# Sliding-window attention feeding a routed expert layer: attention's transfers issued at other places of a step, and the gate's value logits in four matmuls of 128 keys by 64 columns

## The chip, the cores and the metric

The kernel runs on 1 core of one Trainium2 chip. The metric is device time of one execution in microseconds (us). The kernel before takes 1083.74 us, the median of 3 runs (1080.22 to 1085.4).

Names of the engines: PE is TensorE's matmul, PEld its weight load, DVE VectorE, ACT ScalarE, POOL GpSimd; SP is SyncE, which here only issues transfers.

## The reference

Attention over 8 batches, 8 heads, 576 positions of 64 channels, where a query sees the 64 keys up to its own; its output, as 4608 rows of 512 channels, goes through a layer of 8 experts, of which each row uses the two with the highest noisy logits.

```python
scores = q @ k.T / sqrt(64)                       # only 0 <= query - key < 64 count
attn = softmax(scores);  x = attn @ v             # all float32
logits = x @ w_gate + log1p(exp(x @ w_noise)) * noise
top2, weights = softmax over the two largest logits of a row
out[row] += weight * (relu(x[row] @ w1[e]) @ w2[e])     # for both experts e of the row
```

## The kernel before

**Two stages.** Attention runs in NT = 36 steps of one Python loop (`for j in range(NT + 3)`, three more to drain it), and after it the experts run over lists of rows: for each expert three chunks of 384, 448 and 384 rows, first an up product (`up`), then a down product (`down`), each float32 value split into two parts that the fast matmul form takes. Every engine executes its instructions in the order in which the program emits them, so the order of the calls in the loop is the order on each engine. Nothing else schedules.

**A step of attention.** Step j has one block of 64 positions (i = j // 4) of one pair of batches (bp = j % 4), all 8 heads. In the loop's order: `scores(j)` (PE, queries by keys of this block and the one before), `soft_b(j-1)` and `soft_a(j)` (ACT: the exponential, and a copy out of PSUM), `pv(j-2)` (PE, probabilities by values), `norm_b(j-3)` (ACT, 8 scaled copies), `soft_max(j)`, `soft_max2(j)` (DVE, then POOL's subtraction), `transp(j-1)` (PE), `logits(j)` (PE), `apply_mask(j-1)` (DVE) and `logits_copy(j)` (ACT). On PE a step from the fifth on is 16 matmuls of scores, 32 of pv, 4 transposes and 8 of logits; float32 matmuls, transposes aside, are executed as two passes, each with a weight load of its own, so that the profile counts 32, 64, 4 and 16.

**Logits through the values.** The gate's logits x @ [w_gate, w_noise] need x, but x = attn @ v, so the program multiplies the values by the gate first. `logits(j)` takes the transposed values of the step (`vt`, 128 channels of two heads by four blocks of 128 keys) as the stationary operand and the gate's columns (`wgx_sb`) as the moving one: for each block and each half a of its keys a matmul with 64 stationary columns and 32 moving ones, into 64 of the 128 partitions of a PSUM tile `ps_g` (`VG`). Two places of 128 columns alternate between steps. `logits_copy(j)` copies 128 x 128 values from there into slot 4 of the value tile `vw`, and `pv` two steps later multiplies all of `vw` by the probabilities. `ps_g` is also where the routing's small matmuls go (`rank`, `reserve`).

**Transfers.** A step loads queries (`qc`), keys (`KW`), values (`vw`) and transposed values (`vt`), 256 KB each (values 272 KB), and stores one block of rows (`xrows`, 256 KB). All are issued by SP from one queue, in order; SP stops at a transfer until its own conditions hold, and what stands behind it waits with it. Every transfer also waits for the landing of the one eight places before it. At the head of step j stand the loads of queries and keys for step j+3 and of `vt` for step j+2, then `store(j-4)`, then at some steps one of five small things (`REST`), and at steps 2, 4, 6 and 8 a quarter of the first expert's weights (`load_w1`, 512 KB). The values for step j+2 stand behind `pv(j-2)`, which frees their place. `qc` has four buffers, `vt` three.

**After attention** the rows' slots are scattered and rows gathered by POOL (`scatter`, `gather`), which drains a list of such calls, two or three a step (`drain_slots`).

Of the kernel before, what the change touches and what calls it, by code (L numbers as in the profile page):

```python
# [8 lines left out]
F32 = mybir.dt.float32  # L9
# [4 lines left out]
AF = mybir.ActivationFunctionType  # L14
# [3 lines left out]
B, H, S, D = 8, 8, 576, 64  # L18
N, DM, E, F = 4608, 512, 8, 1024
NB = S // 64  # L20
NP = B // 2
NT = NP * NB
KD, KF = DM // 128, F // 128
# [11 lines left out]
W1G = 12  # L35
# [28 lines left out]
def tile_kernel(ctx, tc, qT, kT, vx, vT, wgx, noise, w1, w2, out):  # L64
    nc = tc.nc
# [14 lines left out]
    acon = at.enter_context(tc.tile_pool(name="acon", bufs=1))  # L80
    ld = at.enter_context(tc.tile_pool(name="ld", bufs=2))
# [3 lines left out]
    KW = acon.tile([128, NP, 2, H, 64], F32)  # L85

    VW = [acon.tile([128, 2, 5, 2, 4, 17], F32, name=f"vw{j}") for j in range(NP)]
    QC, VT = {}, {}

    def load_qk(j):  # L90
        i, bp = divmod(j, NP)
        QC[j] = ld.tile([128, H, 64], F32, name="qc", bufs=4)
        nc.sync.dma_start(QC[j], qT[bp, :, i])
        nc.sync.dma_start(KW[:, bp, i % 2], kT[bp, :, i])


    def load_v(j):
        i, bp = divmod(j, NP)
        nc.sync.dma_start(VW[bp][:, i % 2, 0:4], vx[bp, i])


    def load_vt(j):
        i, bp = divmod(j, NP)
        VT[j] = ld.tile([128, 4, 128], F32, name="vt", bufs=3)
        nc.sync.dma_start(VT[j], vT[bp, i])

    for j in range(2):
        load_qk(j)
    wgx_sb = acon.tile([128, 4, 32], F32)
    nc.sync.dma_start(wgx_sb, wgx)  # L110
    load_vt(0)
    load_v(0)
    load_qk(2)
    load_vt(1)
    load_v(1)
    load_qk(3)

    ones = acon.tile([128, 128], F32)
    nc.vector.memset(ones, 1.0)

    idle = ps.tile([128, 512], F32, name="ps_g")

    def warm(n):
        for _ in range(n):
            nc.tensor.matmul(idle[:, 384:512], lhsT=ones, rhs=ones, start=True, stop=True)
# [43 lines left out]
    def load_pads(q):  # L169
        if q == 0:  # L170
            o = LIST * 2
            for n in CHUNKS:
                w = n // 32 * 2
                nc.sync.dma_start(rows(L, o, [[w, 32], [LIST * 2, E - 1], [1, w]]),
                                  pad_f[:, None, :w].to_broadcast([32, E - 1, w]))
                o += n * 2
            return
        pad_t = pad_o.rearrange("k p c -> k (p c)")
        if q == 1:
            nc.sync.dma_start(rows(L, 0, [[256, CAP // 128], [1, 256]]), pad_t[:CAP // 128])  # L180
            nc.sync.dma_start(rows(L, CAP // 128 * 256, [[256, 1], [1, CAP % 128 * 2]]), pad_t[:1, :CAP % 128 * 2])
        else:
            nc.sync.dma_start(rows(L, CAP * 2, [[256, OVT], [LIST * 2, E], [1, 256]]),
                              pad_t[:, None, :].to_broadcast([OVT, E, 256]))

    REST = [lambda: nc.sync.dma_start(noise_sb, noise), lambda: nc.sync.dma_start(X[0:DUMP, :], zero),
            lambda: load_pads(0), lambda: load_pads(1), lambda: load_pads(2)]
# [5 lines left out]
    w1s = wts.tile([128, KD, F], F32)  # L193
# [2 lines left out]
    w1l = wts.tile([128, KD, F], F32R)  # L196
    W2 = {}

    def load_w1(e, ks=slice(0, KD)):
        if e < E:  # L200
            nc.sync.dma_start(w1s[:, ks], w1[e][:, ks])

    def load_w2(e, ks=slice(0, KF)):
        if e < E:
            nc.sync.dma_start(w2s[:, ks], w2[e][:, ks])
# [10 lines left out]
        return [lambda f=f: split(w2s[:, f], W2["h"][:, f], W2["l"][:, f]) for f in range(KF)]  # L216


    VG = idle[:, 0:256].rearrange("p (n c) -> p n c", n=2)

    def logits(j):
        p = VG[:, j % 2]
        x = VT.pop(j)
        for u in range(2):
            for g in range(2):
                for a in range(2):
                    q = u * 2 + g
                    nc.tensor.matmul(p[a * 64:a * 64 + 64, q * 32:q * 32 + 32], lhsT=x[:, q, a * 64:a * 64 + 64],
                                     rhs=wgx_sb[:, g * 2 + a, :], start=True, stop=True)

    def logits_copy(j):
        i, bp = divmod(j, NP)
        nc.scalar.activation(VW[bp][:, i % 2, 4, :, :, 0:16].rearrange("p u k e -> p (u k) e"),
                             VG[:, j % 2].rearrange("p (k e) -> p k e", e=16), AF.Copy)

    ST, T, P, TP, PT, XT = {}, {}, {}, {}, {}, {}

# [340 lines left out]
    def turn(e, c):  # L578
        pool = (exa, EXB.get("p"))[work.index((e, c)) % 2]
        xh = pool.tile([128, KD, WIDE], F32R, name="xh")  # L580
        xl = pool.tile([128, KD, WIDE], F32R, name="xl")
        XH[e, c], XL[e, c] = xh, xl
        cur = {}

        def f(q, m):
            if e:
                y = exa.tile([128, m // 32, KD, 32], F32, name="xy", bufs=2)
                nc.vector.transpose(y.rearrange("p t k c -> p (t k c)"),
                                    XG[e, c, q][:, :m // 32].rearrange("p t d -> p (t d)"))
                cur[q] = y.rearrange("p t k c -> p k t c")  # L590
            else:
                y = turn_bank()[:, :KD * m].rearrange("p (k m) -> p k m", k=KD)
                for k in range(KD):
                    nc.tensor.transpose(y[:, k], XG[e, c, q][:m, k * 128:k * 128 + 128], ident[:m, :m])
                cur[q] = y.rearrange("p k (t c) -> p k t c", c=32)

        def g(q, m):
            h, l = (x[:, :, q * 128:q * 128 + m].rearrange("p k (t c) -> p k t c", c=32) for x in (xh, xl))
            nc.scalar.activation(h, cur[q], AF.Copy)  # L599
            nc.vector.tensor_tensor(l, cur[q], h.bitcast(F32), op=OP.subtract)  # L600
        return [lambda q=q, m=m, x=x: x(q, m) for q, m in tiles(c) for x in (f, g)]
# [90 lines left out]
    def drain(n):  # L692
        calls[0] += 1
        while n and pending and calls[0] > calls[1]:
            f = next(pending[0], None)
            if f == HOLD:
                calls[1] = calls[0] + f
            elif f:
                f()
                n -= 1  # L700
            else:
                pending.pop(0)
# [5 lines left out]
    def drain_slots(n):  # L708
        for f in slots[:n]:
            f()  # L710
        del slots[:n]
# [4 lines left out]
    def ahead(n):  # L716
        for _ in range(n):
            if j >= NT and len(taken) < AHEAD:
                next(up00)
                taken.append(1)  # L720


    def rate(q):
        n = next(b for a, b in RATE if j < a)
        return (q + 1) * n // SLOTS - q * n // SLOTS
# [5 lines left out]
    def on(f, j, *a):  # L731
        if 0 <= j < NT:
            f(j, *a)

    for j in range(NT + 3):
        if j == TURN:
            for q, f in enumerate(turn(0, 0)):
                aux.setdefault(j + q // 2, []).append(f)
        if 0 < j < NT - 3:
            load_qk(j + 3)  # L740
        if j < NT - 2:
            load_vt(j + 2)
        if j < 2:
            load_v(j + 2)
        on(store, j - 4)
        if 2 < j < 3 + len(REST):
            REST[j - 3]()
        if W1G - 8 <= 2 * j < W1G - 8 + 4 * KD and j % 2 == 0:
            k = (j * 2 - W1G + 8) // 4
            load_w1(0, slice(k, k + 1))  # L750
        if NT - 2 <= j < NT + 2:
            load_w2(0, slice((j - NT + 2) * 2, (j - NT + 3) * 2))
        on(norm_a, j - 3)
        drain(rate(0))
        on(scores, j)
        on(soft_b, j - 1)
        on(soft_a, j)
        ahead(2)
        drain(rate(1))
        on(pv, j - 2)  # L760
        on(norm_b, j - 3, 0)
        on(soft_max, j)
        on(soft_max2, j)
        drain_slots(1)
        if j < NP:
            warm(WARM)
        on(transp, j - 1)
        ahead(2)
        on(logits, j)
        on(norm_b, j - 3, 1)  # L770
        on(apply_mask, j - 1)
        drain(rate(2))
        on(logits_copy, j)
        ahead(2)
        on(gate, j - 3)
        drain(rate(3))
        drain_slots(1 + j % 2)
        for f in aux.get(j, ()):
            f()
        drain(rate(4))  # L780
# [13 lines left out]
    for n, (e, c) in enumerate(work):  # L794
# [29 lines left out]
        if last and e + 1 < E:  # L824
            side += split_w1() + [lambda: load_w1(e + 2)]
# [5 lines left out]
        if n == 1:  # L831
            load_w1(1)
# [62 lines left out]
    with tc.If(ntot > 0):  # L895
# [4 lines left out]


_INS = {"qT": [NP, 128, NB, H, 64], "kT": [NP, 128, NB, H, 64], "vx": [NP, NB, 128, 4, 2, 4, 17],
        "vT": [NP, NB, 128, 4, 128], "wgx": [128, 4, 32], "noise": [128, NT, E], "w1": [E, 128, KD, F], "w2": [E, 128, KF, DM]}


def layout(inputs):
# [46 lines left out]
```

## Time and profile before

| what | value |
|---|---|
| median of 3 runs | 1083.74 us |
| the profiled execution | 1081.11 us, of which its span is 1079.3 us |
| PE busy over the span | 1004.2 us, 93% |
| PE matmuls, and as many weight loads | 8313 |
| DVE, ACT, POOL busy | 444.0, 391.4, 534.3 us |
| attention, to the last transposes of its loop | about 190 us |

The page gives one profiled execution. Times in rows are microseconds from the span's start. In a group of instructions, "out<-in" are the program's names, the number after x is the count, then busy time, mean of one in nanoseconds, and idle time of the engine just before those instructions with what ended it. "issue" as the one who ended an idle time means that the engine waited for nothing that the profile shows. Matmuls are pipelined, so the busy time of neighbours overlaps, and the pace is read from the starts.

### The profile page before, as it was taken

The numbers are of one execution on the slowest core, as the hardware profiler recorded it, in microseconds if no ns is written. First come the engines' busy times: TensorE is split into PE (matmuls) and PEld (weight loads), VectorE is DVE, ScalarE is ACT, GpSimd is POOL, SyncE is SP. The second block draws the span as 40 slices with busy tenths as digits, with TensorE's granted clock in tenths as the row PEclk, the third lists the DMA queues.
The fourth block names the chain that finished last, engine by engine and source line by source line (L and its number), as shares of the span: only waits on it lengthen the run. The fifth ranks groups of instructions, "written<-read, shape, count | busy, mean of one in ns | idle before, by whom it ended". The sixth has DMA issues, their size and how long they took to land. (4 is left out here: it accounts for less than half of the span.)

```text
span 1079.3 us, 20457 instructions
## 1 busy us (share of the span) xinstructions
PE 1004.2 (93%) x8313; PEld 894.3 (83%) x8313; DVE 444.0 (41%) x943; ACT 391.4 (36%) x975; POOL 534.3 (50%) x612
## 2 busy tenths in 40 slices
PE   8778777899969999999999999999999999999994
PEld 7667566778859888988898988898889888998893
DVE  6687768531234224422543253326232623352220
ACT  4775656521233224322432252225222522342220
POOL 4435636664276524653465446544555454554411
PEclk9998989999989999999999999999999999999997
DMA  9998988498634324423442345234422542233212
GB/s 347 331 324 225 253 222 245 102 252 177 188 118 132 57 39 125 132 50 42 120 132 49 44 118 136 46 52 123 128 48 46 156 102 42 47 54 51 39 22 32
DMA packets 62681, 133.45 MB, mean 124 GB/s; under 512 B 16776, under 2 KB 17266, under 8 KB 60786
## 3 DMA queue, kind: packets, MB, share of 16 engines
q1 hardware_dynamic: 39986, 92.11, 26.9%
q0 software_dynamic: 22592, 39.95, 21.5%
q8 instruction: 67, 1.10, 0.4%
q14 instruction: 36, 0.29, 0.1%
HBM read 92.31 MB, written 39.70 MB: 122 GB/s over the span
## 5 line engine op out<-in xcount | busy, mean ns | idle before, releaser
L573 POOL DMA_INDIRECT xg<-xrows,ixs x266 | 258.6, 972 | 81.1 <-issue 74.7
L640 PE MATMUL ps_u<-xh,w1h 128*128 128x384 f32 (+1 forms) x752 | 260.7, 347 | 11.5 <-ACT xh L599 10.3
L641 PE MATMUL ps_u<-xl,w1h 128*128 128x384 f32 (+1 forms) x752 | 260.5, 346 | 0.0
L642 PE MATMUL ps_u<-xh,w1l 128*128 128x384 f32 (+1 forms) x752 | 260.1, 346 | 0.0
L655 POOL DMA_INDIRECT out_dram<-yo,lts x70 | 111.6, 1594 | 298.9 <-ACT yo L675 154.0
L670 PE MATMUL ps_d<-w2h,hh 128*128 128x512 f32 x576 | 224.7, 390 | 0.0
L672 PE MATMUL ps_d<-w2h,hl 128*128 128x512 f32 x576 | 224.5, 390 | 0.0
L671 PE MATMUL ps_d<-w2l,hh 128*128 128x512 f32 x576 | 224.4, 390 | 0.0
L647 DVE SCALAR_TENSOR_TENSOR hl<-ps_u,hh 128x384 fp32r<-128x384 f32 x188 | 104.7, 557 | 270.9 <-ACT hh L646 270.9
L646 ACT ACTIVATE hh<-ps_u 128x384 fp32r<-128x384 f32 x188 | 92.4, 492 | 240.7 <-PE ps_u L642 240.5
L640 PEld LDWEIGHTS ps_u<-xh,w1h 128*128 128x128 f32 x752 | 142.1, 189 | 17.3 <-ACT xh L599 11.2
L641 PEld LDWEIGHTS ps_u<-xl,w1h 128*128 128x128 f32 x752 | 141.9, 189 | 5.2 <-DVE xl L600 0.7
L642 PEld LDWEIGHTS ps_u<-xh,w1l 128*128 128x128 f32 x752 | 141.9, 189 | 3.7
L670 PEld LDWEIGHTS ps_d<-w2h,hh 128*128 128x128 f32 x576 | 108.1, 188 | 22.8 <-issue 1.1
L672 PEld LDWEIGHTS ps_d<-w2h,hl 128*128 128x128 f32 x576 | 108.1, 188 | 22.6
L671 PEld LDWEIGHTS ps_d<-w2l,hh 128*128 128x128 f32 x576 | 108.1, 188 | 21.8
L675 ACT ACTIVATE yo<-ps_d,lts 128x512 f32<-128x512 f32 x63 | 43.4, 688 | 194.9 <-PE ps_d L672 115.4
L600 DVE TENSOR_TENSOR xl<-xy,xh 128x512 fp32r<-128x512 f32 (+1 forms) x70 | 46.7, 667 | 147.7 <-ACT xh L599 147.7
L475 POOL DMA_INDIRECT slots<-val,posi x72 | 70.1, 974 | 18.6 <-issue 14.1
L316 PE MATMUL ps_o<-vw,pt 64*64 64x85 f32 x2176 | 56.7, 248 | 21.4 <-issue 20.2
L281 POOL TENSOR_TENSOR t<-t,mx 128x512 f32<-128x512 f32 x36 | 37.5, 1042 | 78.0 <-DVE mx L280 74.5
L316 PEld LDWEIGHTS ps_o<-vw,pt 64*64 64x64 f32 x2176 | 51.3, 143 | 25.4 <-issue 23.9
(145 smaller groups left out, 950.1 us busy)
## 6 DMA issues: line engine op xcount, KB each, us to landing
w2s<-in_w_dram SPq DMA_DIRECT2D x7, 2048.0 KB
w1s<-in_w_dram SPq DMA_DIRECT2D x7, 2048.0 KB
vw<-in_vx_dram SPq DMA_DIRECT2D x36, 272.0 KB
out_dram<-zero SPq DMA_DIRECT2D x37, 256.0 KB
qc<-in_qT_dram SPq DMA_DIRECT2D x36, 256.0 KB
KW<-in_kT_dram SPq DMA_DIRECT2D x36, 256.0 KB
vt<-in_vT_dram SPq DMA_DIRECT2D x36, 256.0 KB
xrows<-x SPq DMA_DIRECT2D x36, 256.0 KB
```

Of the source, the lines that this page charges most:

```text
L316: nc.tensor.matmul(PO[j][u * 64:u * 64 + 64, a, g * 2 + x, :], lhsT=pt[pa, w, u * 2 + g, x * 64:x * 64 + 64], rhs=v[pa, (i + w) % 2, :, u, ...
L475: s = nc.gpsimd.indirect_dma_start(out=L, out_offset=bass.IndirectOffsetOnAxis(ap=posi[:, c2, q:q + 1], axis=0), in_=val[:, c2, q, :], in_ ...
L573: nc.gpsimd.indirect_dma_start(out=XG[e, c, t // 4][:, t % 4, :], out_offset=None, in_=XQ[:(DUMP + seen.get((e, c), NT) * 128) * 4], in_of ...
L640: nc.tensor.matmul(p[:, :n], lhsT=w1h[:, k, fs], rhs=xh[:, k, :n], start=(k == 0), stop=False)
L641: nc.tensor.matmul(p[:, :n], lhsT=w1h[:, k, fs], rhs=xl[:, k, :n], start=False, stop=False)
L642: nc.tensor.matmul(p[:, :n], lhsT=w1l[:, k, fs], rhs=xh[:, k, :n], start=False, stop=(k == KD - 1))
L646: nc.scalar.activation(h, p[:, :main], AF.Relu)
L647: nc.vector.scalar_tensor_tensor(l, p[:, :main], 0.0, h.bitcast(F32), op0=OP.max, op1=OP.subtract)
L655: nc.gpsimd.indirect_dma_start(out=out[:DUMP + seen.get((e, c), NT) * 128], out_offset=bass.IndirectOffsetOnAxis(ap=LT[e, c][:m, q, 0:1], ...
L670: nc.tensor.matmul(p, lhsT=hh[f][:, sl], rhs=w2h[:, f, :], start=(f == 0), stop=False)
L671: nc.tensor.matmul(p, lhsT=hh[f][:, sl], rhs=w2l[:, f, :], start=False, stop=False)
L672: nc.tensor.matmul(p, lhsT=hl[f][:, sl], rhs=w2h[:, f, :], start=False, stop=(f == KF - 1))
```

## The change

**Logits.** One matmul for each block of 128 keys, with all 128 as the stationary columns and 64 moving columns, those of both halves. Half of the result is not wanted; the two copies take the wanted halves, one for each half of the partitions. There is one place of 256 columns instead of two of 128. `wgx_sb` holds the same numbers in another shape.

**Transfers.** Of step j's head only the keys and the store are left. The queries for step j+3 are issued behind `scores(j)`, the transposed values for j+2 behind `logits(j)`, `qc` has three buffers and `vt` two, so both loads now take the place that the matmuls just before them have read. The quarters of the weights become halves of quarters (256 KB) at steps 2 to 9, behind the queries.

```diff
+    def load_q(j):
+        i, bp = divmod(j, NP)
+        QC[j] = ld.tile([128, H, 64], F32, name="qc", bufs=3)
+        nc.sync.dma_start(QC[j], qT[bp, :, i])
+    def load_k(j):
+        i, bp = divmod(j, NP)
+        nc.sync.dma_start(KW[:, bp, i % 2], kT[bp, :, i])
...
-        VT[j] = ld.tile([128, 4, 128], F32, name="vt", bufs=3)
+        VT[j] = ld.tile([128, 4, 128], F32, name="vt", bufs=2)
...
-    VG = idle[:, 0:256].rearrange("p (n c) -> p n c", n=2)
+    VG = idle[:, 0:256].rearrange("p (n c) -> p n c", n=1)
...
-                for a in range(2):
-                    q = u * 2 + g
-                    nc.tensor.matmul(p[a * 64:a * 64 + 64, q * 32:q * 32 + 32], lhsT=x[:, q, a * 64:a * 64 + 64],
-                                     rhs=wgx_sb[:, g * 2 + a, :], start=True, stop=True)
+                q = u * 2 + g
+                nc.tensor.matmul(p[:, q * 64:q * 64 + 64], lhsT=x[:, q, :], rhs=wgx_sb[:, g], start=True, stop=True)
...
-        nc.scalar.activation(VW[bp][:, i % 2, 4, :, :, 0:16].rearrange("p u k e -> p (u k) e"),
-                             VG[:, j % 2].rearrange("p (k e) -> p k e", e=16), AF.Copy)
+        for a in range(2):
+            h = slice(a * 64, a * 64 + 64)
+            nc.scalar.activation(VW[bp][h, i % 2, 4, :, :, 0:16].rearrange("p u (g x) e -> p (u g) x e", x=2),
+                                 VG[h, 0].rearrange("p (k a x e) -> p k a x e", a=2, x=2, e=16)[:, :, a], AF.Copy)
...
         if 0 < j < NT - 3:
-            load_qk(j + 3)
-        if j < NT - 2:
-            load_vt(j + 2)
+            load_k(j + 3)
+        on(store, j - 4)
...
         on(scores, j)
+        if j < NT - 3:
+            load_q(j + 3)
+        if W1G // 2 - 4 <= j < W1G // 2 + 4:
+            k = j - W1G // 2 + 4
+            load_w1(0, slice(k // 2, k // 2 + 1), slice(k % 2 * F // 2, (k % 2 + 1) * F // 2))
+        if 2 < j < 3 + len(REST):
+            REST[j - 3]()
...
         on(logits, j)
+        if j < NT - 2:
+            load_vt(j + 2)
```

SP's order of before around steps 6 and 7 (each row a transfer; "waits PE" or "waits Activation" is a condition on that engine, "DMAHW" one on a landing):

```order
L93 DMA qc<-in_qT_dram 128x512 [waits DMAHW4_49,PE_49]
L94 DMA KW<-in_kT_dram 128x512 [waits DMAHW5_49]
L105 DMA vt<-in_vT_dram 128x512 [waits DMAHW6_49,PE_49]
L338 DMA xrows<-x 128x512 [waits DMAHW7_49,Activation_49]
L180 DMA slots<-pad_o 9x256 [waits DMAHW0_49,Pool_49]
L181 DMA slots<-pad_o 1x128 [waits DMAHW1_49]
L201 DMA w1s<-in_w_dram 128x1024 [waits DMAHW2_49]
L99 DMA vw_90<-in_vx_dram 128x544 [waits DMAHW3_49,PE_49]
L93 DMA qc<-in_qT_dram 128x512 [waits DMAHW4_49]
L94 DMA KW<-in_kT_dram 128x512 [waits DMAHW5_49]
L105 DMA vt<-in_vT_dram 128x512 [waits DMAHW6_49,PE_49]
L338 DMA xrows<-x 128x512 [waits DMAHW7_49,Activation_49]
```

The same place now:

```order
L112 DMA vt<-in_vT_dram 128x512 [waits DMAHW5_49,PE_49]
L97 DMA KW<-in_kT_dram 128x512 [waits DMAHW6_49]
L345 DMA xrows<-x 128x512 [waits DMAHW7_49,Activation_49]
L93 DMA qc<-in_qT_dram 128x512 [waits DMAHW0_49,PE_49]
L208 DMA w1s<-in_w_dram 128x512 [waits DMAHW1_49]
L187 DMA slots<-pad_o 9x256 [waits DMAHW2_49,Pool_49]
L188 DMA slots<-pad_o 1x128 [waits DMAHW3_49]
L106 DMA vw_90<-in_vx_dram 128x544 [waits DMAHW4_49,PE_49]
L112 DMA vt<-in_vT_dram 128x512 [waits DMAHW5_49,PE_49]
L97 DMA KW<-in_kT_dram 128x512 [waits DMAHW6_49]
L345 DMA xrows<-x 128x512 [waits DMAHW7_49,Activation_49]
L93 DMA qc<-in_qT_dram 128x512 [waits DMAHW0_49,PE_49]
```

Before, one transfer of a step (the values, `vw`) and the next step's store wait for an engine and the others follow at once; now the queries, the values, the transposed values and the store each wait for a different place of the step.

PE's order of before in one step (scores, pv, transposes, logits):

```order
L257 MATMUL ps_s<-KW,qc 64x128 [waits DMAHW1_49,DMAHW0_49,DVE_49]
L257 MATMUL ps_s<-KW,qc 64x128 x15
L316 MATMUL ps_o<-vw_90,pt 64x85 [waits DMAHW7_49,DVE_49,Activation_49]
L316 MATMUL ps_o<-vw_90,pt 64x85 x31
L293 MATMUL ps_t<-ident,p 128x128 [waits PE_49,Activation_49]
L293 MATMUL ps_t<-ident,p 128x128 x3
L228 MATMUL ps_g<-wgx_sb,vt 64x32 [waits DMAHW7_49]
L228 MATMUL ps_g<-wgx_sb,vt 64x32 x7
```

and now:

```order
L264 MATMUL ps_s<-KW,qc 64x128 [waits DMAHW1_49,DMAHW0_49,DVE_49]
L264 MATMUL ps_s<-KW,qc 64x128 x15
L323 MATMUL ps_o<-vw_90,pt 64x85 [waits DMAHW6_49,DVE_49,Activation_49]
L323 MATMUL ps_o<-vw_90,pt 64x85 x31
L300 MATMUL ps_t<-ident,p 128x128 [waits PE_49,Activation_49]
L300 MATMUL ps_t<-ident,p 128x128 x3
L234 MATMUL ps_g<-wgx_sb,vt 128x64 [waits DMAHW4_49]
L234 MATMUL ps_g<-wgx_sb,vt 128x64 x3
```

Eight matmuls became four at the same place. On ACT one copy became two at the same place; DVE's and POOL's orders are the same.

## Rows read from the trace of the kernel before

**Rows 1.** Stretches: length, busy time of each engine (count), clock, DMA share, GB/s.

```profile
19.79:171.06 151.27, 115.27 (x3282) 99.81 (x3281) 109.38 (x282) 98.95 (x357) 73.44 (x105) 0.93 0.93 279
25.40:68.40 43.00, 33.46 (x1012) 29.22 (x1012) 32.60 (x73) 32.50 (x118) 20.15 (x25) 0.96 0.98 337
68.40:105.00 36.60, 27.96 (x770) 24.13 (x771) 27.54 (x78) 22.62 (x83) 16.81 (x26) 0.91 0.85 238
400.00:600.00 200.00, 200.00 (x990) 180.19 (x989) 75.24 (x137) 66.01 (x132) 102.75 (x94) 1.00 0.38 90
```

**Rows 2.** Groups by line, PE's matmuls in 19.79 to 171.06 us.

```profile
L316 PE MATMUL ps_o<-vw,pt 64*64 64x85 f32 x1792 | 48.0, 251 | 21.4 <-issue 20.2 <-ACT vw L233 0.7 <-DMA vt<-in_vT_dram 0.2
L257 PE MATMUL ps_s<-KW,qc 64*64 64x128 f32 x903 | 36.1, 292 | 7.7 <-issue 7.7
L228 PE MATMUL ps_g<-wgx_sb,vt 128*64 128x32 f32 x464 | 20.6, 230 | 3.6 <-issue 3.6
```

**Rows 3.** Timeline of PE: start, duration, instruction, count, idle time before it.

```profile
48.53 0.45 PE L257 MATMUL ps_s<-KW,qc 64*64 64x128 f32 x8 [1.77 <-issue]
48.75 1.41 PE L316 MATMUL ps_o<-vw,pt 64*64 64x85 f32 x64
50.09 0.66 PE L293 MATMUL ps_t<-ident,p 128*128 128x128 f32 x4
50.67 0.66 PE L228 MATMUL ps_g<-wgx_sb,vt 128*64 128x32 f32 x16
51.26 1.10 PE L257 MATMUL ps_s<-KW,qc 64*64 64x128 f32 x32
52.42 0.33 PE L316 MATMUL ps_o<-vw,pt 64*64 64x85 f32 x2
53.93 1.40 PE L316 MATMUL ps_o<-vw,pt 64*64 64x85 f32 x62 [1.17 <-issue]
```

**Rows 4.** The page's part 1: busy time, share and instructions of each engine.

```profile
PE 1004.2 (93%) x8313; PEld 894.3 (83%) x8313; DVE 444.0 (41%) x943; ACT 391.4 (36%) x975; POOL 534.3 (50%) x612
```

**Rows 5.** The page's part 3: a DMA queue, its packets, MB, share.

```profile
q8 instruction: 67, 1.10, 0.4%
```

**Rows 6.** Timeline of PE: the transposes of two steps that follow each other.

```profile
88.13 0.66 PE L293 MATMUL ps_t<-ident,p 128*128 128x128 f32 x4
91.51 0.66 PE L293 MATMUL ps_t<-ident,p 128*128 128x128 f32 x4
```

**Rows 7.** Timeline of SP: one step's transfers, start and issue time.

```profile
60.52 0.33 SPq L99 DMA_DIRECT2D vw<-in_vx_dram  x1
60.89 0.43 SPq L93 DMA_DIRECT2D qc<-in_qT_dram  x1
61.38 0.42 SPq L94 DMA_DIRECT2D KW<-in_kT_dram  x1
61.90 0.38 SPq L105 DMA_DIRECT2D vt<-in_vT_dram  x1
62.38 1.23 SPq L338 DMA_DIRECT2D xrows<-x  x1
```

**Rows 8.** Timeline of PE: four transposes with 128 stationary columns, and what follows.

```profile
225.72 0.60 PE L594 MATMUL ps_u<-ident,xg 128*128 128x128 f32 x4
226.07 0.48 PE L670 MATMUL ps_d<-w2h,hh 128*128 128x512 f32 x1
```

**Rows 9.** Timeline of PE: float32 matmuls of 128 by 128 columns, and what follows.

```profile
12.66 1.16 PE L125 MATMUL ps_g<-ones 128*128 128x128 f32 x8
13.65 0.60 PE L293 MATMUL ps_t<-ident,p 128*128 128x128 f32 x4
```

**Rows 10.** Groups by line, ACT in 19.79 to 171.06 us.

```profile
L335 ACT ACTIVATE x<-ps_o,r 128x80 f32<-128x80 f32 x232 | 53.6, 347 | 5.0 <-DVE r L327 4.0 <-DMA xrows<-x 0.5 <-DVE r L326 0.4
L233 ACT ACTIVATE vw<-ps_g 128x128 f32<-128x128 f32 x29 | 8.5, 292 | 26.9 <-PE ps_g L228 25.1 <-remote 1.7
```

**Rows 11.** Waits of the whole run: who waited for whom, total, times, longest.

```profile
PE ps_u L640 <- ACT xh L599: 10.3, 2, 9.3
PE ps_g L455 <- ACT vw L233: 0.8, 2, 0.4
```

More of the change, by code (lines that the diff above doesn't have):

```diff
@@ L88, in tile_kernel @@
     QC, VT = {}, {}
+    def load_q(j):
[5 more added lines that the diff above has]
+        nc.sync.dma_start(KW[:, bp, i % 2], kT[bp, :, i])
     def load_qk(j):
[L91 to L94, printed above, removed]
+        load_q(j)
+        load_k(j)
     def load_v(j):
@@ L108, in tile_kernel @@
         load_qk(j)
-    wgx_sb = acon.tile([128, 4, 32], F32)
+    wgx_sb = acon.tile([128, 2, 64], F32)
     nc.sync.dma_start(wgx_sb, wgx)
@@ L112, in tile_kernel @@
     load_v(0)
+    load_vt(1)
     load_qk(2)
-    load_vt(1)
     load_v(1)
-    load_qk(3)
+    load_k(3)
     ones = acon.tile([128, 128], F32)
@@ L197, in tile_kernel, with load_w1 @@
     W2 = {}
-    def load_w1(e, ks=slice(0, KD)):
+    def load_w1(e, ks=slice(0, KD), fs=slice(0, F)):
         if e < E:
-            nc.sync.dma_start(w1s[:, ks], w1[e][:, ks])
+            nc.sync.dma_start(w1s[:, ks, fs], w1[e][:, ks, fs])
     def load_w2(e, ks=slice(0, KF)):
@@ L216, in split_w2 @@
         return [lambda f=f: split(w2s[:, f], W2["h"][:, f], W2["l"][:, f]) for f in range(KF)]
-    VG = idle[:, 0:256].rearrange("p (n c) -> p n c", n=2)
+    VG = idle[:, 0:256].rearrange("p (n c) -> p n c", n=1)
     def logits(j):
-        p = VG[:, j % 2]
+        p = VG[:, 0]
         x = VT.pop(j)
@@ L739, in tile_kernel @@
         if 0 < j < NT - 3:
-            load_qk(j + 3)
-        if j < NT - 2:
-            load_vt(j + 2)
+            load_k(j + 3)
+        on(store, j - 4)
         if j < 2:
             load_v(j + 2)
[L745 to L750, printed above, removed]
         if NT - 2 <= j < NT + 2:
@@ L902 @@
 _INS = {"qT": [NP, 128, NB, H, 64], "kT": [NP, 128, NB, H, 64], "vx": [NP, NB, 128, 4, 2, 4, 17],
-        "vT": [NP, NB, 128, 4, 128], "wgx": [128, 4, 32], "noise": [128, NT, E], "w1": [E, 128, KD, F], "w2": [E, 128, KF, DM]}
+        "vT": [NP, NB, 128, 4, 128], "wgx": [128, 2, 64], "noise": [128, NT, E], "w1": [E, 128, KD, F], "w2": [E, 128, KF, DM]}
 def layout(inputs):
```

## The prediction, made before the result was known

> **What bounds the kernel now.** I read the stretches first. Among the experts PE is busy for 200.00 of 200 us at full clock and DMA for 0.38 of its time [rows 1]; the change touches nothing there. In attention, from 19.79 to 171.06 us, PE is busy for 115.27 of 151.27 us, and no other engine for more than 109.38 [rows 1]. These are 29 steps (29 copies of the logits [rows 10]), so a step takes 5.22 us. A step without a hole takes 91.51 - 88.13 = 3.38 us [rows 6]. What fills the rest is the question.
>
> The groups by line come next. The idle time before PE's matmuls is 20.2 + 7.7 + 3.6 = 31.5 us of "issue", against 0.2 us of waiting for a load [rows 2]. The data are there; something that the profile doesn't name is not. The timeline shows where the holes stand: one ends at 48.53, the next at 53.93, and between them PE did 8 + 64 + 4 + 16 + 32 + 2 = 126 matmuls [rows 3], each with its weight load: 252 instructions and a few semaphores. The holes wander through the step, so it is no operand that is late. The page has a DMA queue for instructions: 67 packets, 1.10 MB, so 16.4 KB each [rows 5]. PE has 2 x 8313 instructions of these two kinds [rows 4], and 16626 / 67 = 248. So a packet is about 252 to 256 instructions, and PE stops where the next packet of its own program has not landed. The stretch holds 3282 / 126 = 26.0 packets, 5.82 us each. Work for 126 matmuls at the pace without holes is 126 / 116 x 3.38 = 3.67 us, less than the 5.40 us between the two holes of the timeline. The bound of attention is thus the time in which an instruction packet arrives, in a stage whose DMA share is 0.93 [rows 1].
>
> A second loss hangs on the first. The granted clock averages 0.93 [rows 1]; between its two levels, 1.2 and 2.4 GHz, this is 14% of the stretch at the lower, 21 us, which cost at most half, 10.6 us.
>
> The Trainium skill speaks against this reading: "Runtime: NRT & Kernel Launch", section "Instruction fetch mechanics", has a program refilled in blocks of 256 instructions and calls the cost of crossing a block boundary mostly hidden. The block size agrees with the 126 pairs of the timeline; "mostly hidden" does not agree with holes of 1.77 and 1.17 us at two boundaries in a row [rows 3]. By the rule the change's fewer instructions would be worth nothing, which is rival B below.
>
> **Fewer instructions.** Eight matmuls of a step, 16 in the profile's count, become 4, counted 8. So 29 x 8 = 232 of 3282 matmuls go, and as many weight loads: 3050 / 126 = 24.2 packets instead of 26.0. If a packet goes on costing 5.82 us, that is 1.8 x 5.82 = 10.5 us; if only the holes of the missing packets go, 1.8 x 31.5 / 26 = 2.2 us. In between lies what I expect: a packet takes as long to arrive as now, and PE has more work to do meanwhile, 126 / 108 x 3.38 = 3.94 us instead of 3.67. Each of the 21 or so holes that remain is 0.27 us shorter, 5.8 us, and with the 2.2 us this is 8. Term: -8 us, between -10.5 and -2.2.
>
> **The new matmul's own time.** The 16 of before take 51.26 - 50.67 = 0.59 us [rows 3]. No row shows 128 stationary by 64 moving columns. Nearest rows: four transposes with 128 stationary columns take 226.07 - 225.72 = 0.35 us, 88 ns each [rows 8]; eight float32 matmuls of 128 by 128 take 13.65 - 12.66 = 0.99 us, 124 ns each [rows 9]. At the least the new ones go at the old rate per instruction, 37 ns. So eight cost 0.30 to 0.99 us, against 0.59: -0.3 to +0.4 a step. I take 88 ns, since there the weights have the same width and the moving part is short: 0.70 us, +0.11 a step, 3.2 us in all. Most of it lies under the wait for the next packet; only where there is no hole does it lengthen the step. Term: +1 us, between -3 and +11.6.
>
> The Trainium skill, "TensorE: Matmul & The Clock Gate", section "LDWEIGHTS (loading the stationary operand)", gives a weight load its columns divided by 1.2 in ns. For 128 columns that is an estimate of 107 ns, 0.85 us for eight, and the term would be +0.26 a step, +7.5 us if nothing hid it. The 88 ns of the transposes, load and product together, are shorter than the rule's load alone; I go by the row.
>
> **Two copies for one.** The copy of 128 x 128 values takes 292 ns [rows 10]. Each of the two has as many values per partition on half of the partitions: 146 to 292 ns each, so 0 to 0.29 us more a step for ACT; I take 0.29. ACT has 98.95 / 29 = 3.41 us a step [rows 1] and comes to 3.70, below the step. Behind the copies on ACT stand the split of the weights and the next step's exponential; they move by 0.29 us into time in which ACT waits for PE anyway (25.1 us before this copy alone [rows 10]). The routing's matmuls, which write the same PSUM tile, wait for the copy: 0.4 us each now [rows 11], and 0.29 more. The next step's logits stand in the same place, but start a whole step after the copy. Term: +1 us, between 0 and +8 (0.29 x 29).
>
> **The transfers.** Five transfers of a step are issued from 60.52 to 62.38 us [rows 7]: 1.33 MB in 1.9 us, for which the DMA engines need 3.9 us at 337 GB/s [rows 1]. A packet of instructions that is asked for then shares them. Now they leave one by one behind scores, pv, logits and the store's copies. The bytes are the same, so a fetch is quicker only where the engines run empty between two transfers: they have no such gap from 25.40 to 68.40 (share 0.98), some later (0.85) [rows 1]. After the first term 23.5 us of holes and up to 10.6 us of clock are left. I take a sixth of the 34 us: -6, between -34 (no fetch waits any more) and +4 (fetches now meet a transfer in every part of the step). A sixth is nearer to nothing because the share of 0.93 is nearer to full than to empty. The weights in halves are the same bytes and land three steps before their use. The queries leave behind the matmuls that free their place, nearly three steps ahead: nothing. `vt` has the shortest lead and is rival C.
>
> **Sum.** -8 + 1 + 1 - 6 = -12. The profiled execution took 1081.11 us, so it would take 1069.1; it lies 2.6 us under the median of the runs, and the median becomes 1083.74 - 12 = 1071.7 us. Attention's gain reaches the end because the experts follow on the same PE, busy without a gap. The stage between has one long wait, 9.3 us for gathered rows [rows 11]; it hangs on POOL's calls behind attention, and POOL, busy for 73.44 of 151.27 us [rows 1], keeps up with shorter steps.
>
> **Rivals.** A, the bursts are nearly the whole matter: fetches no longer wait, the holes go. A step then ends with DVE, 109.38 / 29 = 3.77 us of work, or ACT, 3.70; with their waits some 4.2, so 29 x 1.0 us is about 30 and the time 1053.7. For it speaks the burst [rows 7], against it the share of 0.98. B, no change: the holes have another cause, or what attention gains is spent in the 9.3 us wait that gets longer. Then the small costs stay, +2, or nothing: 1083.7 to 1086. C, slower: DMA itself becomes the bound. From 68.40 to 105.00 it moved 238 GB/s at a share of 0.85 [rows 1]; if that is all it can do, a step's 1.33 MB take 5.6 us, 0.37 more than a step now, and with `vt` issued only two steps ahead instead of nearly three nothing hides it: 29 x 0.37 = 11 us, 1094.7. It decides from the point where a load of `vt` lands later than two steps less 0.6 us after its issue, 9.8 us at the present pace. Against it speak the 337 GB/s before [rows 1].
>
> **Numbers.** The forecast, a gain of 7 to 23 us (1061 to 1077), has 0.60; A 0.12, B 0.17, C 0.11. A measurement can tell about 0.5%, 5.4 us, from no change. Faster by more: nearly all of the forecast and A, 0.70. Same: B and the forecast's rest, 0.19. Slower: C, 0.11. The range of eight in ten goes from 1055, which takes in part of A, to 1086, which takes in B.
>
> **What would show it.** Right: attention's stretch is shorter by about the sum; the matmuls between two holes are still 126, and they now cover more of a step; PE's "issue" time falls from 31.5 to about 20 us; the clock's mean rises; eight new matmuls start 0.70 us before what follows. The transfers' term is right if SP's issues stand apart and holes shrink by more than 0.27 us each. Wrong: "issue" time as before with fewer packets (then packets cost more), a wait of PE for `vt` or `qc` (C), or a longer wait for gathered rows after attention (B).

## The result, and the profile after

After takes 1078.43 us in the median (1072.76 to 1082.42, 20 runs), before beside it 1083.54 us (1076.76 to 1089.55, 20 runs). The ratio is 0.9946, with a 95% interval of 0.993 to 0.9962: 5.8 us faster, between 4.1 and 7.6. The forecast was 12 us; the sign is right, the size is half. A second comparison, told below, gave 0.9929 (0.99 to 0.9959), 7.7 us. Weighted by the inverse squares of the intervals' widths the two give 0.9942, 6.3 us.

The trace of after is of the longest of its 20 executions, 1082.42 us with a span of 1080.6 us, where before's, 1081.11 us with a span of 1079.3 us, lies under before's median. Totals of these two traces are therefore not set against each other; what one step costs can be. First the page's lines for PE and the instruction queue, as [rows 4, 5]:

```profile
PE 1019.3 (94%) x8025; PEld 914.9 (85%) x8025; DVE 444.4 (41%) x943; ACT 404.0 (37%) x1011; POOL 535.6 (50%) x612
...
q8 instruction: 65, 1.06, 0.4%
```

288 matmuls fewer, 36 x 8, and 65 packets of instructions for 67. Next the first stretch of [rows 1] (length, busy time of PE, PEld, DVE, ACT, POOL with counts, clock, DMA share, GB/s):

```profile
19.79:171.06 151.27, 124.93 (x2964) 114.09 (x2964) 104.93 (x270) 106.39 (x376) 69.37 (x101) 0.88 0.91 269
```

PE is busier in the same stretch with fewer matmuls (124.93 us for 115.27), at a lower clock (0.88 for 0.93). The groups of PE's matmuls there, as [rows 2]:

```profile
L323 PE MATMUL ps_o<-vw,pt 64*64 64x85 f32 x1728 | 46.5, 258 | 19.0 <-issue 14.7 <-ACT w1h L215 2.3 <-ACT vw L240 1.9
L264 PE MATMUL ps_s<-KW,qc 64*64 64x128 f32 x896 | 35.6, 302 | 2.2 <-issue 2.0 <-DVE t L282 0.2
L234 PE MATMUL ps_g<-wgx_sb,vt 128*128 128x64 f32 x221 | 32.3, 296 | 2.9 <-issue 1.7 <-DMA vt<-in_vT_dram 1.1
```

The "issue" time is 14.7 + 2.0 + 1.7 = 18.4 us for 31.5, in 221 / 8 = 27.6 steps for 29: 0.67 us a step for 1.09. That is what was forecast ("about 20 us"). In the whole run PE waits for "issue" 10 times, 19.0 us, before 24 times, 33.6 us: the holes are fewer rather than shorter, as the timeline shows where [rows 3] stood (start, duration, instruction, count, idle time before):

```profile
47.33 0.51 PE L323 MATMUL ps_o<-vw,pt 64*64 64x85 f32 x11 [3.52 <-issue]
47.77 0.66 PE L300 MATMUL ps_t<-ident,p 128*128 128x128 f32 x4
48.26 1.78 PE L234 MATMUL ps_g<-wgx_sb,vt 128*128 128x64 f32 x8
49.97 1.99 PE L264 MATMUL ps_s<-KW,qc 64*64 64x128 f32 x32
51.73 2.49 PE L323 MATMUL ps_o<-vw,pt 64*64 64x85 f32 x64
54.15 1.10 PE L300 MATMUL ps_t<-ident,p 128*128 128x128 f32 x4
55.06 1.03 PE L234 MATMUL ps_g<-wgx_sb,vt 128*128 128x64 f32 x8
```

One hole of 3.52 us, and none at the next border: from 47.33 PE does 11 + 4 + 8 + 32 + 64 + 4 = 123 matmuls and passes the 126th inside the logits at 55.06 without a stop. It worked at half clock there (logits to scores 49.97 - 48.26 = 1.71 us; at full clock 0.94, from 58.72 to 59.66), so the packet had landed when it was wanted: the trace records each packet of the instruction queue, and this one started at 50.67 us and took 0.93 us. A long hole, a lower clock after it, and then a border that costs nothing: here the two losses partly pay for each other.

The same records show what ends a hole. In before's trace the packets that ran from 46.27 to 47.23 us and from 51.72 to 52.68 us stand before the two ends of holes of [rows 3], 48.53 and 53.93 us. Of before's 22 holes of 0.3 us or more from 14 to 175 us that end with "issue", 19 end 1.0 to 1.6 us after a packet has landed, where packets start 5.8 us apart. So the wait for the next packet, which the prediction inferred from the count of 126, stands in the trace.

SP's issues of one step, where [rows 7] shows five within 1.9 us:

```profile
58.36 0.33 SPq L106 DMA_DIRECT2D vw<-in_vx_dram  x1
59.76 0.33 SPq L112 DMA_DIRECT2D vt<-in_vT_dram  x1
60.14 0.42 SPq L97 DMA_DIRECT2D KW<-in_kT_dram  x1
60.65 0.39 SPq L345 DMA_DIRECT2D xrows<-x  x1
61.14 0.38 SPq L93 DMA_DIRECT2D qc<-in_qT_dram  x1
```

Four transfers still leave from 59.76 to 61.14, within 1.4 us (1.4 to 2.6 us in the steps from 30 to 99 us); only the values stand apart, 1.4 us here. `vt` goes when the logits are done; the next step's keys and store, whose conditions hold by then, follow at once, and the queries go when the scores are done, the first thing PE does in a step. On PE the end of the logits and the end of the next scores are 0.9 us apart. The new places are thus neighbours in time, though not in the program.

Last the waits of the whole run (total, times, longest), as [rows 11], and ACT's copies, as [rows 10]:

```profile
PE ps_u L647 <- ACT xh L606: 8.3, 2, 7.3
...
PE ps_o L323 <- ACT w1h L215: 2.3, 3, 0.8
...
PE ps_o L323 <- ACT vw L240: 1.9, 3, 0.8
PE ps_g L234 <- DMA vt<-in_vT_dram: 1.8, 2, 1.1
...
PE ps_g L462 <- ACT vw L240: 1.3, 2, 0.6
...
PE ps_g L389 <- ACT vw L240: 0.6, 1, 0.6
```

```profile
L240 ACT ACTIVATE vw<-ps_g 64x128 f32<-64x128 f32 x56 | 15.3, 274 | 31.2 <-PE ps_g L234 30.7
```

The wait for gathered rows, 7.3 us at the longest for 9.3, is shorter by 2 us, not longer; it differs from run to run (6.3 to 10.3 us in the traces of about 1065 to 1080 us). New are waits for the split of the first weights (`w1h`), 2.3 us, and for `vt`, 1.8 us; those for the copies of the logits sum to 1.9 + 1.3 + 0.6 = 3.8 us, before 0.7 [rows 2], 0.8 [rows 11] and another 0.8.

### The profile page after: what moved, and what is told of

Read it like the earlier page. It is cut to its first block, busy times and chain, and to the rows that moved or that the text cites. A ratio compares the mean times of both kernels' runs of the same rounds, so it can differ in the third digit from the quotient of the medians.

```text
span 1080.6 us, 19954 instructions
## 1 busy us (share of the span) xinstructions
PE 1019.3 (94%) x8025; PEld 914.9 (85%) x8025; DVE 444.4 (41%) x943; ACT 404.0 (37%) x1011; POOL 535.6 (50%) x612
```

## The experiments

Theory 1: the wide logits' own time eats what the fewer packets give, and the spread transfers bring the gain. Theory 2: the wide logits bring it and the transfers nothing. Theory 3: attention gets shorter, but the wait behind it takes the time back.

### Three rounds in which every program took about 1177 us

Four kernels and before took turns in each of these rounds, on a different chip each. Before's own medians there were 1176.96, 1173.95 and 1177.64 us. The parts: the wide logits with the transfers of before; the transfers with the old logits; after; before again; and before with half of its logits, where the keys of a=1 are left out and the PSUM tile is set to zero once at the start,

```diff
-                for a in range(2):
+                for a in range(1):
```

The first round:

> The new logits (four matmuls of 128 keys by 64 columns, one place, two copies) with the transfers of the kernel before. Theory 1, the wide form eats the gain: eight passes at 117 ns (0.94 us a step, as the changed kernel's timeline has it, against 0.59) cost about what the fewer instruction packets bring, so the time is that of the kernel before within 3 us (1081 to 1087), and PE's issue time is some 6 us lower than before. Theory 2, the logits bring what was forecast and the transfers take part of it away: 1073 to 1077. Theory 3, attention is shorter but the wait for gathered rows behind it takes it back: attention's end 5 us or more earlier, total unchanged.

Measured: 1180.33 us, ratio 1.0042 (1.0002 to 1.0082).

> The transfers of the changed kernel with the logits of the kernel before. Theory 1: all of the gain is the transfers', 1074 to 1079, with PE's issue time down by 10 us or more. Theory 2: 1083 to 1088, slower by waits for the transposed values, of which PE shows several us. Theory 3: attention shorter, total unchanged.

Measured: 1177.32 us, 1.0028 (0.999 to 1.0066).

> The changed kernel once more, for a second trace and its times on the chip of the other runs: 1076 to 1081 by any theory; the matmuls of the logits at 0.94 us a step again by theory 1; attention's end against the first trace of it tells how far one trace of this kernel stands from another.

Measured: 1178.55 us, 1.0063 (1.0022 to 1.0104).

> The kernel before once more, for a second trace: ratio 1.000 within 0.004 by any theory; PE's issue time near 33 us if the holes are a property of the kernel, and off by 10 us or more if they are a matter of one execution.

Measured: 1177.49 us, 1.0026 (0.9987 to 1.0065). This is the same kernel as its comparison, so differences of 0.3% mean nothing here. The second round:

> The logits of after with the transfers of before; a second look, since in the first round every kernel took about 1177 us. Theory 1 (the wide logits take 0.94 us a step instead of 0.59, and that eats most of what the fewer instruction packets give; the spread of the transfers brings the rest): ratio to before 0.997 to 1.002, the eight passes at 0.94 us also here, PE's issue time about 5 us under before's 31.5. Theory 2 (the logits bring the gain, the transfers nothing): 0.993 to 0.996. Theory 3 (attention gets shorter but the wait behind it takes it back): the first up matmul 5 us or more earlier than before's, the wait for gathered rows longer, the total the same.

> The transfers of after with the logits of before. Theory 1: 0.993 to 0.997, holes shorter, issue time 20 to 25 us, the logits at 0.59 us a step. Theory 2: 0.999 to 1.002. Theory 3: the total as before with a longer wait behind attention.

> After once more. All theories: 0.993 to 0.997 if the cores run as in the first comparison; its trace is a second one to read the holes, the logits (0.94 us a step by theory 1) and the end of attention from.

> Before with only the first half of the logits' matmuls (the four calls with a=0; the other half of the partitions of the logits stays zero and is left out of the computation). As many PE instructions as after, without the new form's own time: the step loses half of 0.59 us and 1.8 instruction packets. Theory 1: the packets' term is real, so 8 us and up to 29 x 0.29 more: ratio 0.985 to 0.993, issue time under 26 us. Theory 2: 0.990 to 0.996. Theory 3: attention shorter by 8 us or more, the total no more than 0.3% less. If the packets cost what their number is not, issue time stays at 31 us and the ratio at 0.995 or above.

Measured, in this order: 1.0013 (0.9971 to 1.0055), 1.0005 (0.9969 to 1.004), 1.0019 (0.9983 to 1.0055), 0.995 (0.9918 to 0.9983). The third round:

> The logits of after with the transfers of before, on cores that run before in about 1083 us. Theory 1 (the wide logits take 0.35 us a step more than the old ones, which uses up what the fewer packets give): ratio 0.998 to 1.003. Theory 2 (the fewer packets bring the change's gain): 0.993 to 0.996. Theory 3 (the stage behind attention takes the gain back): up matmuls of the first expert earlier, total within 0.2%.

> The transfers of after with the logits of before, on cores that run before in about 1083 us. Theory 1: 0.991 to 0.996, this part brings all of the 5 to 6 us, and without the wide logits a little more. Theory 2: 0.999 to 1.002. Theory 3: total as before.

> Before with only the a=0 half of the logits' matmuls (the other half is left out of the computation): the instruction count of after without the wide form's own time. Theory 1: 0.988 to 0.994, that is 6 us or more under z1, the price of the wide form. Theory 2: at z1 within 0.2%. If the packets' number is worth nothing: 0.997 to 1.000.

> After once more beside the three parts: 0.993 to 0.996 as in the first comparison. Theory 1: the sum of z1's and z2's differences within 0.3%; with a trace for a second reading of the end of attention.

Measured: 1.001 (0.998 to 1.0041), 0.9969 (0.9933 to 1.0005), 0.9985 (0.9945 to 1.0024), 0.9988 (0.9952 to 1.0025).

In these rounds neither the change nor one of its two parts gains anything that can be measured. The timeline of before in the first round shows another kind of loss, which the first trace of before doesn't have: within pv PE gets a few matmuls, then stops for 0.4 us, several times in a row.

```profile
107.19 0.34 PE L316 MATMUL ps_o<-vw,pt 64*64 64x85 f32 x2 [0.41 <-issue]
107.92 0.38 PE L316 MATMUL ps_o<-vw,pt 64*64 64x85 f32 x4 [0.38 <-issue]
108.66 0.38 PE L316 MATMUL ps_o<-vw,pt 64*64 64x85 f32 x4 [0.36 <-issue]
109.41 0.31 PE L316 MATMUL ps_o<-vw,pt 64*64 64x85 f32 x3 [0.37 <-issue]
110.14 1.20 PE L316 MATMUL ps_o<-vw,pt 64*64 64x85 f32 x25 [0.41 <-issue]
```

The new stretch begins every 0.73 to 0.75 us, with 2 to 4 matmuls in it. These stops are not the wait for a packet: of the 39 of 0.3 us or more in this trace from 14 to 175 us, 31 end at other times than 1.0 to 1.6 us after a packet's landing. PE isn't full among the experts either, 192.28 of 200 us where [rows 1] has 200.00:

```profile
400.00:600.00 200.00, 192.28 (x905) 168.37 (x904) 64.09 (x118) 57.16 (x116) 91.37 (x84) 0.97 0.30 67
```

So these rounds can't say where 6 us of 1083 come from, and the parts were run again, each alone beside before.

### What sets the wide form's own time

After with half of the moving columns; the other half of the logits is left out, and the PSUM tile is set to zero once at the start.

```diff
-                nc.tensor.matmul(p[:, q * 64:q * 64 + 64], lhsT=x[:, q, :], rhs=wgx_sb[:, g], start=True, stop=True)
+                nc.tensor.matmul(p[:, q * 64:q * 64 + 32], lhsT=x[:, q, :], rhs=wgx_sb[:, g, 0:32], start=True, stop=True)
```

> After with 32 moving columns instead of 64 in the logits' four matmuls (128 stationary columns as in after; the upper 32 of each 64 result columns stay zero, so half of the logits is left out). For the trace alone: if the width of the stationary operand sets the new form's time, the eight passes take 0.94 us from start to the next matmul, as in after; if the moving columns set it, about 0.6 to 0.7 us (88 ns a pass, the row of the transposes, less a part).

One run of 1081.95 us, before 1083.0 us beside it. From the timeline, logits and scores:

```profile
21.40 0.98 PE L235 MATMUL ps_g<-wgx_sb,vt 128*128 128x32 f32 x8
22.31 0.89 PE L265 MATMUL ps_s<-KW,qc 64*64 64x128 f32 x24
```

Eight passes take 22.31 - 21.40 = 0.91 us with half of the moving columns, 0.94 with all. With the same 32 moving columns and 64 stationary ones eight passes take 0.58 us (the half logits, below). So the time goes with the stationary width far more than with the moving columns, as the first branch had it.

### The transfers alone

Logits, copies and `wgx_sb` of before in after.

> The transfers of after with the logits of before, once more alone beside before (the look at the narrow form ran at 1083 us on its own). Theory 1: 0.991 to 0.996. Theory 2: 0.999 to 1.002. Theory 3: total as before with a longer wait for the gathered rows. Where before takes 1177 us again: 0.997 to 1.003 and nothing is told apart.

Measured: 1075.32 us, before 1078.15 us, ratio 0.998 (0.9957 to 1.0002): 2.2 us, between 4.6 and none. Theory 1's 0.991 to 0.996 is missed. PE's groups in the stretch of [rows 2], and the new wait:

```profile
L323 PE MATMUL ps_o<-vw,pt 64*64 64x85 f32 x1856 | 47.9, 247 | 18.8 <-issue 18.4 <-DVE pt L305 0.2
L264 PE MATMUL ps_s<-KW,qc 64*64 64x128 f32 x936 | 37.1, 290 | 7.7 <-issue 7.4
L235 PE MATMUL ps_g<-wgx_sb,vt 128*64 128x32 f32 x480 | 21.3, 229 | 3.9 <-issue 2.8 <-DMA vt<-in_vT_dram 1.1
```

```profile
PE ps_g L235 <- DMA vt<-in_vT_dram: 2.8, 3, 1.1
```

"Issue" is 28.6 us in 480 / 16 = 30 steps, 0.95 a step for 1.09. In the whole run it is 30.4 us for before's 33.6; the wait for `vt`, 2.8 us in all, gives back most of the difference.

### The wide logits alone

After's `logits`, `logits_copy`, one place and `wgx_sb` in before.

> The logits of after with the transfers of before, alone beside before. The transfers alone gave 0.998, 2.8 us by the medians of that run, where the whole change gave 0.9946. Theory 1 (the wide logits' own time uses up what the fewer packets give): 0.997 to 1.002. Theory 2 (they bring the larger part): 0.994 to 0.997.

Measured: 1071.84 us, before 1078.79 us, ratio 0.9929 (0.9899 to 0.996): 7.7 us, between 4.3 and 10.9. Theory 1 falls and theory 2 holds: this part gives as much as the whole change.

```profile
L316 PE MATMUL ps_o<-vw,pt 64*64 64x85 f32 x1856 | 46.0, 246 | 14.4 <-issue 10.8 <-ACT vw L233 2.0 <-DVE mm L433 1.0
L257 PE MATMUL ps_s<-KW,qc 64*64 64x128 f32 x944 | 37.4, 296 | 4.4 <-issue 4.2 <-DVE t L275 0.2
L227 PE MATMUL ps_g<-wgx_sb,vt 128*128 128x64 f32 x240 | 33.1, 285 | 1.8 <-issue 1.0 <-DMA qc<-in_qT_dram 0.8
```

"Issue" is 16.0 us in 240 / 8 = 30 steps, 0.53 a step for 1.09, and in the whole run 16.4 us for 33.6. One step without a hole, from its timeline:

```profile
53.89 0.66 PE L293 MATMUL ps_t<-ident,p 128*128 128x128 f32 x4
54.38 1.00 PE L227 MATMUL ps_g<-wgx_sb,vt 128*128 128x64 f32 x8
55.32 1.10 PE L257 MATMUL ps_s<-KW,qc 64*64 64x128 f32 x32
56.24 1.36 PE L316 MATMUL ps_o<-vw,pt 64*64 64x85 f32 x64
57.53 0.66 PE L293 MATMUL ps_t<-ident,p 128*128 128x128 f32 x4
```

From transposes to transposes it takes 57.53 - 53.89 = 3.64 us, where [rows 6] has 3.38. So the wide form adds 0.26 us to PE's own work of a step, 9.4 us in 36 steps, and the time fell all the same.

### Fewer instructions without the wide form

Before with half of its logits, as above.

> Before with only the a=0 half of the logits' matmuls (the other half is left out of the computation), alone beside before: the instruction count of after without the wide form's own time. Theory 1: 6 us or more under the wide logits alone, 0.988 to 0.994. Theory 2: within 0.2% of the wide logits alone. If the number of packets is worth nothing: 0.998 to 1.000.

Measured: 1071.44 us, before 1076.77 us, ratio 0.9953 (0.9924 to 0.9982): 5.1 us, between 1.9 and 8.2.

```profile
L317 PE MATMUL ps_o<-vw,pt 64*64 64x85 f32 x1856 | 49.8, 257 | 19.4 <-issue 14.9 <-ACT w1h L209 2.7 <-DVE pt L299 0.8
L258 PE MATMUL ps_s<-KW,qc 64*64 64x128 f32 x940 | 37.4, 296 | 7.7 <-issue 6.5 <-DVE t L276 0.9
```

As many instructions as after. But the 8 passes that are left take no less time than the 16 of before, as a step without a hole shows:

```profile
86.11 0.66 PE L294 MATMUL ps_t<-ident,p 128*128 128x128 f32 x4
86.70 0.65 PE L229 MATMUL ps_g<-wgx_sb,vt 128*64 128x32 f32 x8
87.28 1.10 PE L258 MATMUL ps_s<-KW,qc 64*64 64x128 f32 x32
89.49 0.66 PE L294 MATMUL ps_t<-ident,p 128*128 128x128 f32 x4
```

From logits to scores it takes 87.28 - 86.70 = 0.58 us for 0.59 [rows 3], and the step 89.49 - 86.11 = 3.38 us as in [rows 6]. A pass takes 73 ns here and 37 ns where both halves alternate; why was not tried. So the expectation that the step loses half of 0.59 us was wrong, and the run is a cleaner test than was meant: fewer instructions at the same own time gave 5.1 us.

Against the wide form PE's own step has 3.64 - 3.38 = 0.26 us less work, 9.4 us in 36 steps, and the program isn't faster: the ratios are 0.9953 and 0.9929, and their intervals leave the half logits at most some 2 us ahead. "Issue" is 21.4 us in 29 steps, 0.74 a step, more than the 0.53 with the wide form (21.4 and 16.4 us in the whole runs). So of the 9.4 us some 5 go into waits for the packet; the rest is not in these waits, and the granted clock, 0.976 in the mean of these runs for 0.982 with the wide form, is enough for it (see the clock, below). Theory 1's "6 us or more under the wide logits" is missed. (In the second and third round at 1177 us the half logits stood 0.6 and 0.3% under the wide ones; there PE's own work may count.)

### The whole change again

> After once more, alone beside before. The wide logits alone gave 0.9929 and the transfers alone 0.998. If the parts add: 0.988 to 0.994. If the transfers bring nothing, or take a little, once the wide logits have shortened the holes: 0.993 to 0.997, as in the first comparison (0.9946), with PE's issue time at 15 to 20 us and 2 to 4 us of waits for vt and for the splitting of the weights that the wide logits alone do not have.

Measured: 1070.59 us, before 1078.61 us, ratio 0.9929 (0.99 to 0.9959): 7.7 us, between 4.4 and 10.8. The gains of the parts, 7.7 and 2.2, don't visibly add, but the intervals are too wide to say that they don't. This trace (span 1068.8 us) is from nearer its median than the first of after:

```profile
L323 PE MATMUL ps_o<-vw,pt 64*64 64x85 f32 x1856 | 46.8, 247 | 16.8 <-issue 10.7 <-DVE r L333 2.4 <-ACT vw L240 1.4
L264 PE MATMUL ps_s<-KW,qc 64*64 64x128 f32 x961 | 36.5, 290 | 2.8 <-issue 2.0 <-DVE t L282 0.8
L234 PE MATMUL ps_g<-wgx_sb,vt 128*128 128x64 f32 x240 | 33.4, 287 | 0.9 <-issue 0.8
```

```profile
PE ps_u L647 <- ACT xh L606: 8.4, 2, 7.3
...
PE ps_g L234 <- DMA vt<-in_vT_dram: 0.3, 1, 0.3
```

"Issue" is 13.5 us in 30 steps, 0.45 a step; `vt` is waited for once, 0.3 us; the rows that are gathered for 7.3 us again. Against the wide logits alone the spread takes 0.08 us a step from the holes, 2.0 us in the whole run (14.4 for 16.4). Theory 3 falls too: the first up matmul starts at 183.31 us for 187.64 in before's trace, and the last down matmul at 1052.56 for 1062.88, so what attention gains, 4.3 us between these two traces, is not taken back behind it. The other 6 us between them arise after the first up matmul: before's trace has a wait of 2.4 us for gathered rows that the other lacks, and 9.3 us for 7.3 at the long one. With one trace of each that can't be put down to the change.

### `vt` back at the head

```diff
-        VT[j] = ld.tile([128, 4, 128], F32, name="vt", bufs=2)
+        VT[j] = ld.tile([128, 4, 128], F32, name="vt", bufs=3)
...
             load_k(j + 3)
+        if j < NT - 2:
+            load_vt(j + 2)
         on(store, j - 4)
...
         on(logits, j)
-        if j < NT - 2:
-            load_vt(j + 2)
```

> After with the load of vt back at the head of the step, behind the keys and with three buffers as before; queries, store and weights stay spread. If the late vt is what keeps the transfers from bringing more (PE waited 2.8 us for vt in the trace of the transfers alone, 1.8 us in the first trace of after, 0.3 us in its second): no wait for vt in the trace, issue time at 13 to 18 us, ratio 0.989 to 0.993. If the packets' arrival does not depend on how the transfers are spread once the logits are short: as after, 0.992 to 0.996. If the burst at the head is what delays the packets: issue time back at 16 us or more and 0.993 to 0.997.

Measured: 1068.91 us, before 1078.33 us, ratio 0.9918 (0.9893 to 0.9943): 8.8 us, between 6.1 and 11.5.

```profile
L323 PE MATMUL ps_o<-vw,pt 64*64 64x85 f32 x1920 | 47.9, 245 | 15.8 <-issue 11.3 <-ACT w1h L215 1.5 <-ACT vw L240 1.5
L264 PE MATMUL ps_s<-KW,qc 64*64 64x128 f32 x972 | 36.6, 282 | 4.0 <-issue 3.1 <-DVE t L282 0.9
L234 PE MATMUL ps_g<-wgx_sb,vt 128*128 128x64 f32 x248 | 31.3, 269 | 1.7 <-issue 1.4 <-DMA vw<-in_vx_dram 0.3
```

"Issue" is 15.8 us in 248 / 8 = 31 steps, 0.51 a step, no better than after's 0.45, and the wait for `vt` is 0.2 us in the whole run. The first branch (no wait for `vt`, 13 to 18 us of issue time, 0.989 to 0.993) fits best, the second isn't excluded. This kernel has the best ratio of all, but its interval reaches over those of after and of the wide logits alone; which of the three is the fastest stays open.

## Why the prediction was off

**The step that failed is the transfers' term.** It said -6 us, "a sixth of the 34 us". The transfers alone gave -2.2 us (between -4.6 and +0.2). On top of the wide logits they gave 6.3 - 7.7, that is +1.4 us, with an uncertainty of some 3.6. With -2 in the place of -6 the sum is -8, and the two comparisons gave -5.8 (-7.6 to -4.1) and -7.7 (-10.8 to -4.4). Four things stand behind it. The text had the transfers "leave one by one behind scores, pv, logits and the store's copies"; four of the five still leave within 1.4 to 2.6 us, since these places are neighbours on the clock. The spread brought the wait for `vt`, 2.8 us in one trace and 0.3 to 1.8 in those of after; the text had it in rival C only, as all or nothing. And the 34 us of which a sixth was taken were too many: 23.5 us of holes were to be left by the fewer packets, and the wide logits alone left 16.0. The clock, up to 10.6 of the 34 us, was counted here too, and it rose with the wide logits and not with the transfers alone (see the clock). How much each of the four is worth wasn't separated.

**Fewer instructions, own time and copies: right in sum.** -8 + 1 + 1 = -6 was forecast, -7.7 (-10.9 to -4.3) measured. The two sizes inside were off, in opposite directions, so that the sum fits is in part luck. The new matmuls' own time was taken from the transposes at 88 ns a pass, +0.11 us a step; it is 0.94 us for the eight, 117 ns a pass, and the step without a hole is 0.26 us longer. The Trainium skill's rule that was weighed there (in "TensorE: Matmul & The Clock Gate", "LDWEIGHTS (loading the stationary operand)": columns divided by 1.2, in ns) gave an estimate of +0.26 a step and of 107 ns a pass. The step agrees, the parts don't: the pass took 117 ns, so the eight took 0.94 - 0.59 = 0.35 us more, and 0.09 of it came back because the logits start 0.49 us after the transposes for 0.58 in [rows 3]. The transposes were the wrong neighbour: what they share with the new form is the width, but they are one call after another into one tile, for which 88 ns held. Against this the holes shrank far more than by 8 us: in the whole run from 33.6 to 16.4 us, by 17.2. With 9.4 us of own work and 1.5 us for the copies that makes -6.3 by the two traces, near the measured -7.7. That fewer packets shorten the time doesn't rest on this sum: the half logits, with the own time of before, gave 5.1 us.

**What hid the own time.** The text said that most of it lies under the wait for the next packet. The half logits bear it out in part: 9.4 us less of PE's work than the wide form has, with as many instructions, made nothing faster. From the third step's logits to the 31st's a step took 5.05 us with the wide logits and 5.09 with the half ones, and by the records of the instruction queue packets started 6.14 and 6.13 us apart there (5.82 in before), though PE's own work differs by 0.26 us a step. So in attention a step lasted about as long as the packets took to come. These are single traces, and the half logits' is also the one at the lower clock in attention, 0.89 for 0.92; how much of the own time lies under the wait and how much the clock gave back wasn't separated.

**The copies** take 274 ns each for the 292 of one, +0.26 us a step for ACT, and PE's waits behind them rose from 2.3 to 3.8 us in the whole run, 1.5 us for the forecast +1.

**The rivals.** A didn't come: holes of up to 3.5 us are left. B's longer wait for gathered rows didn't come either; it is 7.3 us in both traces of after, for 9.3. B's other half, that the holes have another cause, is against the runs: fewer instructions with more work took 7.7 us off, and 19 of before's 22 holes end just after a packet's landing. The Trainium skill's "Runtime: NRT & Kernel Launch", "Instruction fetch mechanics", with its mostly hidden crossing, does not agree with that run. C was right about `vt` as the transfer with the shortest lead, and wrong about its size.

**The clock** was to rise. In the stretch of [rows 1] it is 0.88 and 0.92 in the two traces of after, for 0.93, and with long holes left PE falls to the lower level after them as before. But before's trace is of an execution with a high clock, 0.979; in the last five comparisons, before's 77 executions have 0.965 to 0.981. In the mean of whole executions the clock did rise with the wide logits: from 0.973 to 0.982 alone, from 0.974 to 0.981 in the whole change, and from 0.974 to 0.982 with `vt` at the head. With the transfers alone and with the half logits it stayed (0.976 and 0.975; 0.976 and 0.976). Between levels of 1.2 and 2.4 GHz a rise of 0.009 is some 19 us less at the lower one, worth at most half of that: an estimate of up to 9 us, as much as the whole gain. So a part of what the wide logits gained may have come through the clock; how large it is, and why the half logits didn't raise it, stays open.

## What to carry to other kernels

Where the idle time of an engine is "issue" and returns after a fixed number of instructions, count instructions, not work: fusing small matmuls into wider ones gained 7.7 us here though each step's own work on TensorE grew by 0.26 us. Don't take a matmul's time for a fixed price either: leaving out every second one of before's logits took nothing off the step. Before giving a gain to transfers that are spread over program places, put these places on the timeline: if the engine passes two of them within a microsecond, the burst is still there. And divide a loss among the parts of a change in order, each from what the one before leaves.

## What the runs showed of the hardware

In three rounds, on three chips, where five programs took turns, before took 1174 to 1178 us in the median; in six, on six chips, where two took turns, 1077 to 1083 us. The chip that the results call 5 is in both sets, with 1176.96 and 1078.33 us, so it isn't the chip alone. In the trace of the first such round the first up matmul starts 23 us later than in the first trace of before (211.02 us for 187.64), and the stops of 0.4 us after each few matmuls are in it. What makes PE stop there was not tried, nor which number of programs it takes.
